# Ten attention heads instead of six with a second set of raw queries, and three operations placed elsewhere

## The chip, the cores and the metric

The kernel runs on one core of a Trainium2 chip. The metric is the device time of one execution in microseconds. TensorE (PE) multiplies matrices into eight PSUM banks of 128 x 512 floats; VectorE (DVE), ScalarE (ACT) and GpSimd (POOL) work element by element; SyncE (SP) and POOL issue transfers between on-chip memory and DRAM. Each engine takes its instructions in the order in which the program issues them, and waits at the first that isn't ready.

## The reference

One sequence of 2048 tokens of width 448 goes through an attention block with 16 heads of 28 columns and through a gated feed-forward block with a hidden width of 1792. A gate for each token mixes the two:

```python
qkv = (x @ wqkv).reshape(B, S, 3, H, Dh)
scores = einsum("bhqd,bhkd->bhqk", q, k) * Dh ** -0.5
a = softmax(scores) @ v ; a = a.reshape(B, S, D) @ wo
gate = x @ W_gate ; gate = gate * (gate > 0)
b = (gate * (x @ W_up)) @ W_down
g = sigmoid((x * gate_w).sum(-1))
out = g * a + (1 - g) * b
```

All is in 32-bit floats. Most products are made of a high part (rounded) and a low part (the rest), so that eleven matmuls (L116) stand for one product over 448 columns.

## The kernel before, in words

**Three stages.** The first (up to L635) splits x and the weights into high and low parts, makes queries, keys and values, writes them to DRAM, and begins on the row maxima. The second (L787 to L887) has 32 rounds, two for each head: an even round takes the first eight of the head's 16 blocks of 128 keys, an odd round the other eight. The third (from L893) is the rest of the feed-forward block, the output projection, and the result.

**A round's work.** Scores are made with keys in the partitions and 512 queries along the row (L309). The exponential needs each query's maximum first. For most queries the maxima come from a second, transposed product, queries by keys (`smax`, L282): one matmul for each 128 queries and 512 keys, and a maximum along the row on DVE (L284). They are made a head or so ahead. At the end of a head's maxima, `smax_end` transposes them on PE (L295), copies them on ACT (`mr`, L305), splits them into a high part on ACT (`mh`, L178) and a low part on DVE (`mh`, L184, by `low`), and SP writes both into two extra rows of the queries (L303), so that the score product subtracts them.

**Raw queries.** The last 512 queries (j = 3) go another way in every head but the first. Their raw scores for a round are made in the round before it, copied from PSUM by ACT (L321; in two late rounds by DVE, L319), and DVE keeps a running maximum over the key blocks (`raw_max`, L324). `raw_top` (L330 to L346) then makes one row of it on DVE, sends it through DRAM (`mr_d`) and spreads it over all partitions. In the round itself POOL subtracts it from each raw block (`raw_less`, L350) and ACT takes the exponential in place (`raw_exp`, L354). An odd round rescales what the even round has summed by a factor (`factors`, L369). In the heads of `WIDE` (L113) the odd round treats a second set of 512 queries (j = 2) in the same way: 16 raw blocks instead of eight, whose raw scores stand in the even round, and eight scores fewer in the odd one. Such a head needs only half of the maxima for its rows u from 8 to 11 (`parts_of`, L271), eight `smax` fewer.

**Products with v.** Each round ends with 64 matmuls of probabilities and values (`pv`, L728), four at a time in quarters of PE's columns, into bank 3. DVE copies the bank (L732) or adds it (L734). After an odd round POOL sends the row sums to DRAM and back in another shape (`ls`, L737). In the next even round, at the tenth score, DVE takes their reciprocals (`row_sums`, L745), and SP writes and spreads them (`spread`, L753). At the end of that round POOL multiplies (`normalise`, L758), and the normalised head goes to DRAM (`o_d`).

**Gate and up products.** Between these, PE works on the gate and up products of the feed-forward block (L690), in tiles of 2 x 11 matmuls. 55 of 56 tiles are made in the rounds, two in most and one in some; the hidden tile goes to DRAM (`h_d`, L712). Weights of the first 14 tiles are split by ACT and POOL in the early rounds.

**The order.** It is written out by hand in `ROUNDS` (L49), one string a round; a letter is an operation, a digit its bank: `s` a score and its exponential, `m` a row maximum, `r` a raw score and its copy, `d` a running maximum, `e` a raw exponential, `x` one gate-up matmul (20 of a tile's 22 stand in the string). The loop at L805 issues them one by one. `smax_end` of a head is issued at a round's start: the transpose and the copy at once, the split and the two transfers after the third and fourth score (L811). `raw_less` of all raw blocks is issued before the first letter (L799).

**The end.** After the last round one gate-up tile is left (`gate_up`, L954). The list `todo` (L1013) gives the order: that tile, the last head's row sums and spread, the splitting of wo (`split_wo`, L908), then 56 steps of the down product (`down`, L998; 12 matmuls of L985 a step), with `normalise` before step 3, the fetch of the normalised heads (`or`, L917) before steps 3, 8, 21 and 35, their splitting (`on`), and the output projection (`wout`, L939) in between. Each step fetches the h tile (and in the first 14 the w_down tile) four ahead (`fetch_d`, L964) and splits those two ahead on ACT and DVE (`split_d`, L972). For the last head, the row sums, the spread and the writing go over POOL's queue (`side`, L739).

Of the kernel before, what the change touches and what calls it, by code (L numbers as in the profile page):

```python
# [22 lines left out]
H = 16  # L23
# [34 lines left out]
    ("xxm0s7xm2s3m6xs7r1xm3s0m6s2xm1s3s7m0r6m2s1dm3xs7xxs0xm6s1r2m7xr3xs6xs1xxr0ddm6s7xr2dm3m1s6xxxxds7em0xm1xexm2"
     "m7xs3xs1xexm2xs3m7m1exs2xm0s3xexr1m2xs3m0xxs2xdxm0m3xxem1r2dxs0"),
    ("xr0xs7m2s1xm6s3xxxs0s2m3r1m7m6xs0xds3xs7xm0xs2m3s6xs7s1s2s3m6xxr7m1s0xds6em3r2xm1xxm7ds6r0s3xxxdxxs7em1m3xm2"  # L60
     "s0s7xxm1xexr3dxs2m0xxs1xexxr2edexxm3xxr0xdxs2"),
    ("xs1s0m6xs7m2xm1r3xr7m0s2xr3s1dm6xxr2s0dds7r1m6xxr3s0xds2dxs7r6xxxxm2s0s1xxs7xds0em3s6m2s7exm0xs1em3xs2m0xm7x"
     "m3xs0m1xs2em7xm0m3s1xxs2m7m0xm1xm2m3xxxs0xxexm1exm0r2xm3m1xxds0"),
    ("xs0r1m2s7m6xr3m0dxs1s2s6s7m0xxs3m1xm2xr0m6s1xdr7m2s3s6xdxs1m0xr2m3s6dxs7xs1xs0m3xs2r6m7m1s3xs0m2s7xs3r1dm0xd"
     "s2xexm3r7m6s0s2ds1e"),
    ("xs7s0m2s6xm1r3s7xm0m2s1s6xm3r0xs1xm7r2m6s3m1ds0r7xxxs3dr1xxs0s2ds3xm7r6m0dxxs2s3r1m7xs0xm6s2m7xr3xs6ds0m2dxx"
     "r1xdexxxr2s0xxr3dm7dxs1xs2xm0xs1m3r2xr0dxr1dr3xexxxxxr0ds2xexddm1"),
    ("xm7xr0m1r6m3xds2s7m0xs1xm2xs3s6m7xs0s1m3xxr6m2dm0xxs1r3xm2xr6xr1ds0xm2s7xxxxddxm3es0xs2m7xs1xm0xxem7m1exs3ee"
     "xem0xm2xs3xm0xm1xr2xxxxxdem0xr1m3s2xdxem0"),
# [1013 lines left out]
```

## Time and profile before

| | |
|---|---|
| median of 3 runs | 1237.44 us (1236.15 to 1240.22) |
| profiled execution | 1242.08 us, its span 1240.3 us |
| mean granted clock of TensorE | 0.992 |
| DMA queues 1 and 0 | 37.7% and 9.9% of 16 engines' span |
| row maxima on DVE (L284) | 736, 478.0 us busy |
| exponentials of scores on ACT (L311, into P) | 728, 403.1 us |
| gate and up matmuls (L690) | 1232, 404.1 us |
| raw subtractions on POOL (L350) | 288, in two groups of 211.3 and 150.8 us |

The profile lists for each engine the time in which some instruction of it was busy, for groups of instructions (source line, engine, tiles) their number, busy time and mean length, and the idle time of the engine just before them with what ended it. PE's instructions overlap: a matmul's row is longer than the distance to the next one. A row of a timeline gives start, length, engine, line, tiles and number of merged instructions; a row by stretch gives start and end of the stretch, its length, the busy time and number of instructions of each engine, the granted clock, DMA's share and rate.

### The profile page before, as it was taken

How to read it: one execution, taken by the hardware profiler on the slowest of the kernel's cores; microseconds unless marked ns; L12 is line 12 of the kernel's file. 1: busy time of each engine (PE TensorE's matmuls, PEld its weight loads, DVE VectorE, ACT ScalarE, POOL GpSimd, SP SyncE). 2: the span in 40 equal slices, each digit the busy share in tenths (PEclk: the TensorE clock that was granted, in tenths of full speed). 3: DMA queues.
4: the chain of work that ended last, by engine and by line, in shares of the span. 5: the costliest groups of instructions: out<-in, count | busy, mean ns of one | idle time of the engine just before them, and what ended most of it. 6: DMA issues, size and time to landing. Idle time of an engine off the chain costs nothing.

```text
span 1240.3 us, 18786 instructions
## 1 busy us (share of the span) xinstructions
PE 1214.4 (98%) x6399; PEld 868.3 (70%) x6399; DVE 922.1 (74%) x1622; ACT 816.6 (66%) x1615; POOL 548.8 (44%) x545
## 2 busy tenths in 40 slices
PE   9999999999979999999999999999999999899998
PEld 6888766666646666666666676666666666889997
DVE  6488876877787988889788888888888871543342
ACT  5312666788848787877888787878787885522121
POOL 4232325456553464374448454643738564400000
PEclk9999999999989999999999999999999999899999
DMA  8956736263627353435643443554342422753432
GB/s 305 345 209 247 249 130 214 84 195 99 210 68 250 106 163 100 131 125 163 202 155 108 155 127 106 164 158 144 122 163 86 149 88 81 244 180 110 137 105 77
DMA packets 68275, 193.99 MB, mean 156 GB/s; under 512 B 14850, under 2 KB 21602, under 8 KB 63754
## 3 DMA queue, kind: packets, MB, share of 16 engines
q1 hardware_dynamic: 55188, 148.02, 37.7%
q0 software_dynamic: 12560, 44.32, 9.9%
q8 instruction: 50, 0.82, 0.3%
q10 hardware_dynamic: 432, 0.46, 0.1%
q14 instruction: 45, 0.37, 0.1%
HBM read 132.09 MB, written 61.11 MB: 156 GB/s over the span
## 4 chain that ended last, share of the span: by engine, by line
PE 85%; DMA 6%; DVE 3%; POOL 2%; ACT 2%; issue 1%; SPq 0%; POOLq 0%; DVEq 0%; ACTq 0%
PE b L690 20%; PE b L728 17%; PE b L282 12%; PE b L309 12%; PE b L985 9%; PE b L503 5%; PE b L317 5%; DMA ls<-os 3%; PE b L521 3%; PE b L944 3%; POOL V L350 1%; DVE mx L284 1%; POOL wg L187 1%; DVE mh L184 1%; DMA or<-o_d 1%
## 5 line engine op out<-in xcount | busy, mean ns | idle before, releaser
L284 DVE TENSOR_REDUCE mx<-b 128x1 f32<-128x512 f32 x736 | 478.0, 684 | 44.6 <-PE b L282 40.0
L311 ACT ACTIVATE P<-b 128x512 f32<-128x512 f32 x728 | 403.1, 613 | 96.8 <-PE b L309 93.3
L690 PE MATMUL b<-X,wg 128*128 128x512 f32 (+1 forms) x1232 | 404.1, 401 | 0.3 <-POOL wg L187 0.3
L282 PE MATMUL b<-K,Q 128*128 128x512 f32 x736 | 281.1, 395 | 4.0 <-DVE mx L284 2.8
L309 PE MATMUL b<-Q,K 128*128 128x512 f32 x736 | 272.8, 395 | 3.6 <-DVE mx L284 2.6
L690 PEld LDWEIGHTS b<-X,wg 128*128 128x128 f32 (+1 forms) x1232 | 219.3, 188 | 69.9 <-issue 23.8
L350 POOL TENSOR_TENSOR V<-V,P 128x512 f32<-128x512 f32 x168 | 211.3, 1299 | 35.3 <-DMA P<-mr_d 17.4
L728 PE MATMUL b<-P,v 128*32 128x512 f32 x1696 | 226.3, 594 | 0.0
L712 POOL DMA_DIRECT2D h_d<-rl x56 | 31.3, 559 | 328.6 <-DVE rl L706 321.3
L309 PEld LDWEIGHTS b<-Q,K 128*128 128x128 f32 x736 | 139.0, 189 | 39.2 <-DVE mx L284 5.3
L282 PEld LDWEIGHTS b<-K,Q 128*128 128x128 f32 x736 | 138.6, 189 | 39.5 <-DVE mx L284 7.9
L324 DVE TENSOR_TENSOR P<-b,P 128x512 f32<-128x512 f32 x231 | 155.4, 681 | 11.0 <-ACT V L321 4.6
L350 POOL TENSOR_TENSOR P<-P,P 128x512 f32<-128x512 f32 x120 | 150.8, 1293 | 23.5 <-DMA P<-mr_d 18.5
L728 PEld LDWEIGHTS b<-P,v 128*32 128x32 f32 x1696 | 62.5, 110 | 124.6 <-issue 114.8
L985 PE MATMUL b<-WD,hh 128*128 128x448 f32 x672 | 142.9, 373 | 4.3 <-issue 3.8
L985 PEld LDWEIGHTS b<-WD,hh 128*128 128x128 f32 x672 | 128.2, 191 | 18.0 <-issue 4.1
L317 PE MATMUL b<-Q,K 128*128 128x512 f32 x288 | 111.8, 396 | 8.4 <-DVE mx L284 8.4
L728 PE MATMUL b<-V,v 128*32 128x512 f32 x352 | 114.4, 594 | 0.0
L178 ACT ACTIVATE hh<-hr 128x512 fp32r<-128x512 f32 x56 | 35.3, 631 | 113.3 <-PE b L985 112.6
L321 ACT ACTIVATE V<-b 128x512 f32<-128x512 f32 x160 | 93.6, 613 | 11.7 <-PE b L317 10.8
L354 ACT ACTIVATE V<-V 128x512 f32<-128x512 f32 x168 | 97.8, 663 | 0.0
L184 DVE TENSOR_TENSOR hh<-hr,hh 128x512 fp32r<-128x512 f32 x56 | 38.8, 693 | 63.4 <-ACT hh L178 63.1
(103 smaller groups left out, 1092.0 us busy)
## 6 DMA issues: line engine op xcount, KB each, us to landing
wg<-wgs_d SPq DMA_DIRECT2D x42, 896.0 KB
K<-qk_d SPq DMA_DIRECT2D x64, 224.0 KB
Q<-qk_d SPq DMA_DIRECT2D x64, 224.0 KB
h_d<-rl POOLq DMA_DIRECT2D x56, 256.0 KB, 3.8
hr<-h_d SPq DMA_DIRECT2D x56, 256.0 KB
wgs_d<-wg SPq DMA_DIRECT2D x14, 896.0 KB
qk_d<-st POOLq DMA_DIRECT2D x21, 512.0 KB, 4.7
wgr<-wgu SPq DMA_DIRECT2D x13, 512.0 KB
```

The costliest lines, as they stand in the source:

```text
L282: nc.tensor.matmul(ps, Q[h][:, u * P:(u + 1) * P], K[h % 3][:, c * TB:(c + 1) * TB], start=True, stop=True)
L284: nc.vector.tensor_reduce(MX[h][:, at:at + 1], ps, axis=AX.X, op=OP.max)
L309: nc.tensor.matmul(ps, K[h % 3][:, kt * P:(kt + 1) * P], Q[h][:, j * TB:(j + 1) * TB], start=True, stop=True)
L311: nc.scalar.activation(prob(i, j), ps, AF.Exp, scale=SCALE)
L317: nc.tensor.matmul(ps, K[h % 3][:, kt * P:(kt + 1) * P], Q[h][:, j * TB:(j + 1) * TB], start=True, stop=True)
L321: nc.scalar.activation(own, ps, AF.Copy)
L324: nc.vector.tensor_tensor(run(3 - j), ps, run(3 - j) if i % 8 > 1 else prob(i - 1, j), op=OP.max)
L350: nc.gpsimd.tensor_tensor(own, own, top(3 - j), op=OP.subtract)
L354: nc.scalar.activation(own, own, AF.Exp, scale=SCALE)
L690: nc.tensor.matmul(ps, WS[i][rows, s, a], xf(i // NF, b)[rows], start=(n == 0), stop=(n == NT - 1))
L728: nc.tensor.matmul(po[32 * j:32 * j + 32], VH[h][:, i % NK], prob(i, j), start=(i == i0), stop=(i == i0 + ni - 1))
L985: nc.tensor.matmul(ACC[i // NF][t][:, :D], HH[i][:, a, t * P:(t + 1) * P], WD[:, f, b], start=(f == 0 and n == 0), stop=(f == NF - 1 and n ...
```

## The change

`WIDE` grows from heads 4, 6, 8, 10, 12, 13 to heads 4 to 13. The strings of rounds 1 to 31 are all new; round 0 keeps its own. Counted over all strings, `s` goes from 720 to 688, `m` from 636 to 604, `r` from 288 to 320, `d` from 252 to 280, `e` from 138 to 154, and `x` stays at 1100. Rounds 10, 14, 18 and 22, now of wide heads, hold one gate-up tile instead of two, and the odd rounds after them two instead of one. Eight of the 32 fewer `m` are missing in round 5; the other 24 in rounds 10 to 23, six in each pair of rounds. The ten odd rounds from 9 to 27 now share one string (23 m, 16 s, 8 r, 40 x):

```diff
-WIDE = (4, 6, 8, 10, 12, 13)
+WIDE = (4, 5, 6, 7, 8, 9, 10, 11, 12, 13)
 # round 10
-    ("xs0m6s1m2r7xs0m3s1xs6m2m7r3xxdxs0r1m2s6xr3xdm7xxs0xds2s6r7xm3xm1ds0xs2s3m6xs1xs7m0xem6m3s2s1xxm7m6em2s3r0m1x"
-     "s7xs3dxr2xxs1xds7em3exm0xm1xm7s3xm0exm2r1m3xxxs0xdxxm2exm0xxm1xm2"),
+    ("s6s7m2s0m1s6xs3m2r7m0xr6m1r3m2s7m0r6xr1xds2r7dxs0xr3dxxxs6ds2r0dm1xs7m6xr3xdr1ds2s7xm6xds3s0m6s7m2s3s0m1r6xm"
+     "7s2ds3m0xr1s7xm2dr3xs6m0r7dxr2exr1ds6edees0d"),
```

The low part of the maxima goes to POOL, and all of `smax_end` is issued at the round's start:

```diff
             act_high(mh[:, 0], mr)
-            low(mh[:, 1], mr, mh[:, 0])
+            pool_low(mh[:, 1], mr, mh[:, 0])
...
-            rest = smax_end(min(M), banks[6])
-            rest.pop(0)()
+            for part in smax_end(min(M), banks[6]):
+                part()
```

The reciprocal of the row sums and its spread come at the sixteenth score of an even round:

```diff
-                if ns == 10 and r % 2 == 0 and h:
+                if ns == 16 and r % 2 == 0 and h:
                     row_sums(h - 1)
                     spread(h - 1)
```

In the end, row sums and spread come before step 1, the splitting of wo before steps 2 and 3, `normalise` and the first fetch of `or` before step 4; the first two pairs of w_down and h tiles are fetched before wo, and, as `start` is counted from `todo`, the first pair is split before the last gate-up tile:

```diff
-    todo = [(gate_up, done), (row_sums, H - 1), (spread, H - 1)] + [(gate_up, i) for i in range(done + 1, NB * NF)]
+    todo = [(gate_up, i) for i in range(done, NB * NF)]
...
-    before(3, (normalise, H - 1))
-    for tb, load, split, at in ((0, 3, (9, 10), (12, 12, 13, 13)), (1, 8, (12, 14), (17, 18, 19, 20)), (2, 21, (23, 25), (28,) * 4),
+    before(1, (row_sums, H - 1), (spread, H - 1))
+    before(4, (normalise, H - 1))
+    for c in range(4):
+        before(2 + c // 2, (split_wo, c))
+    for tb, load, split, at in ((0, 4, (9, 10), (12, 12, 13, 13)), (1, 8, (12, 14), (17, 18, 19, 20)), (2, 21, (23, 25), (28,) * 4),
...
-    todo[3:3] = [(split_wo, c) for c in range(4)]
-    load_wo()
     for i in range(4):
         fetch_d(i)
+        if i == 1:
+            load_wo()
```

More of the change, by code (lines that the diff above doesn't have):

```diff
@@ L58 @@
[L58 to L69, printed above, removed]
@@ new lines @@
+    ("xr7r1m0m6s2dxm3xs0r7xdm6xs1xs0m3xxs1r2m0r6xs3r1xdxs7xxdxs2dm3r6exxxs0xm7s3s1xds2m0em7s3xm1xxs0m2xs7m3s1xm2m0"
+     "es7xs3xs1m2s7xm3m0s1s2xem7m3xxm0s1m2xxm3xm1xr0xxdxexem2xs3xm0m1"),
+    ("xm7s2xm1s0xs6xm2s7m3s0xs6m1r7s2m3r0xm1s6r7s3s2dxm1xxs6s0xdm3s1m2r7m6xs0xs3xdm2s6m1r0s7m3xs2r6dxs1m7r3xds2s0x"
+     "m7xm1r6xs2xds0s7ede"),
+    ("xxr1m6s0xm7m3s2r1xr0xs6dm2s7dxxs3xxr1s7m6xxs2dm0m3s7es6xs1xm2m7xs3m0s6xxm2s1xem7m3s0m2xs6m7s1xs3m0xxs1m2xm3x"
+     "s7xm1s0xm3m7exm2s0xr3xxds1m0r2xxxdxs1em3m0xr2xdxr3xem1ds0xxm2ex"),
@@ new lines @@
+    ("xxs7m0xs2s1s6xm7xxs2s1m3s0s7m6r2xm1xxs0s3m6xr7s2r0xxm6ds1ds3xxs2m6er1xxs7xxxs0dxs3s2xes1m0xxxr3s7dxs2xr0xxxx"
+     "xedr3xeexs1dxxr0xxxm2s3xeds1x"),
+    ("xr0s1m7s2m6m3xxs1s7m0xm2s3m1xs7xm0s3r6m1xm7xxds0xs3s2xm7es1m6xr3xm7s2m0dxs6xxs7m1m0s2xxm7s6xm3r0dxs7r1xxem2s"
+     "3m7xxdxs2xm0s7m3xr2m1xm7er0xr3s1xxdexxexxs2xddm0xexm1xm2s3s0xm1"),
+    ("xm7s2xm1s0xs6xm2s7m3s0xs6m1r7s2m3r0xm1s6r7s3s2dxm1xxs6s0xdm3s1m2r7m6xs0xs3xdm2s6m1r0s7m3xs2r6dxs1m7r3xds2s0x"
+     "m7xm1r6xs2xds0s7ede"),
+    ("xs6r2m0s1r7m3xxr6xs2m1s0ds7xxs2xm0s1s7m3m6r2xs0m1s3dxxs7m6s0m1xr2xr7ds6dxs1m0xr3xexxr6ds1m2dxr7s0dxxm3r2xs1x"
+     "s0xs7xs1dm3m0r2dexr7xxds1xxs3r2m0xm1xexr3dxr0xxxddr2s1xm3xxm0xds1"),
@@ new lines @@
+    ("xs2m0m1r7s6xxm3m2r0ds7xxxs1xm2xr3s7m0xds6xr1xs0xds7s6m2xm0r3xm1xs2xs6dxm7s1m0m3r2xm7xxr0xm3xdxxxm1s3dexexm7x"
+     "xm2r3s1xs0xdxem2eexm1m3xxxxexm0em2xs3m1xe"),
+    ("xs6m1r7xm0r2xs3m7r1m6s2xr0dxs7xs2s3xdm6xs0m7s2m1s3r6xm7xdxs2m3r0s1xxr2dr6ds7dxxr0xm1dxm3s2xs7xs6m1r2xs7m0xds"
+     "3xm1s7xm0exr3xs2xs1dm7s0xr2xs1r3dexxxxdxm0s1r2xxr3xdxxr1dxdexm2s0"),
+    ("xs2m0m1r7s6xxm3m2r0ds7xxxs1xm2xr3s7m0xds6xr1xs0xds7s6m2xm0r3xm1xs2xs6dxm7s1m0m3r2xm7xxr0xm3xdxxxm1s3dexexm7x"
+     "xm2r3s1xs0xdxem2eexm1m3xxxxexm0em2xs3m1xe"),
@@ new lines @@
+    ("xs2m0m1r7s6xxm3m2r0ds7xxxs1xm2xr3s7m0xds6xr1xs0xds7s6m2xm0r3xm1xs2xs6dxm7s1m0m3r2xm7xxr0xm3xdxxxm1s3dexexm7x"
+     "xm2r3s1xs0xdxem2eexm1m3xxxxexm0em2xs3m1xe"),
+    ("r7r2m0r6s1m3s2xdm7r0r3s1xxddxr2s7m6xr1xdr0dxs6xr7xdm2s3xr6s1xdr0dxs3m2xdr7ds6xs1xs2m3m0s7s1m3s6m2s7m0s1xs6m2"
+     "s3m7r0xm6s1s2m3s7xxs6r1dm2m3exdr0r6s7edees2d"),
+    ("xs2m0m1r7s6xxm3m2r0ds7xxxs1xm2xr3s7m0xds6xr1xs0xds7s6m2xm0r3xm1xs2xs6dxm7s1m0m3r2xm7xxr0xm3xdxxxm1s3dexexm7x"
+     "xm2r3s1xs0xdxem2eexm1m3xxxxexm0em2xs3m1xe"),
@@ L111 @@
+    ("xxs0xs1xs3xxxs6s2s0s3xxxxs7s2s0s1xxs3xxxs6xs2xs7xxs1s3exxs0s2xxxxexs1s3xs0xexxxexxexxs2s0exxxx"),
 ]
-WIDE = (4, 6, 8, 10, 12, 13)
+WIDE = (4, 5, 6, 7, 8, 9, 10, 11, 12, 13)
 TERMS = [(0, 0), (3, 0), (1, 1), (4, 1), (2, 2), (5, 2), (6, 3), (0, 4), (1, 5), (2, 6), (6, 7)]
```

75 lines of the change are left out of this document (30 added, 45 removed).

## The prediction

> **What bounds the kernel now.** I read the page first, then the busy times by stretch. A stretch here is a round: from the first pv matmul (L728) of one round to the first of the next.
>
> ```profile
> span 1240.3 us, 18786 instructions
> PE 1214.4 (98%) x6399; PEld 868.3 (70%) x6399; DVE 922.1 (74%) x1622; ACT 816.6 (66%) x1615; POOL 548.8 (44%) x545
> ```
> ```profile
> core 0: us, PE busy (x) PEld busy (x) DVE busy (x) ACT busy (x) POOL busy (x), PEclk, DMA share, GB/s
> 192.93:227.64 34.71, 32.81 (x169) 21.80 (x168) 26.12 (x52) 24.33 (x50) 17.51 (x19) 0.95 0.57 199
> 251.47:285.14 33.67, 31.78 (x170) 21.13 (x168) 25.83 (x49) 27.74 (x56) 16.98 (x18) 1.00 0.54 173
> ...
> 345.43:379.65 34.22, 25.86 (x138) 16.55 (x137) 28.95 (x39) 19.63 (x43) 16.34 (x16) 0.85 0.42 142
> ...
> 494.18:524.92 30.74, 30.74 (x168) 21.45 (x166) 25.19 (x48) 26.86 (x54) 11.37 (x10) 1.00 0.41 126
> 524.92:552.67 27.75, 27.75 (x159) 18.33 (x157) 24.92 (x45) 21.23 (x44) 19.63 (x17) 1.00 0.36 119
> 552.67:583.36 30.69, 30.69 (x170) 20.87 (x169) 27.46 (x51) 26.21 (x51) 16.05 (x15) 1.00 0.54 164
> ...
> 998.87:1019.16 20.29, 20.29 (x121) 12.82 (x119) 14.00 (x28) 17.17 (x35) 12.33 (x11) 1.00 0.27 86
> ```
> ```profile
> 552.74 7.00 PE b L728 x64
> ```
>
> The rows are rounds 2, 4, 7, 12, 13, 14 and 30. PE is busy all through rounds 12 to 14, so a round is as long as its matmuls. Counting the letters s, m, r and x in the order strings gives 98, 87 and 100 of them, beside 64 pv matmuls in 7.0 us (the piece of the chain). Round 14 against round 13: (30.69 - 27.75) / (100 - 87) = 0.226 us for one matmul. It is issued at that pitch, though a row calls one 0.39 us long. So a round needs 7.0 + 0.226 x letters + about 0.5 for each gate-up tile. For 98 letters and two tiles that is 30.15, and round 12 has 0.6 over it; for 100 letters 30.6, and round 14 has 0.1. Three rounds lie far above: round 2 (99 letters, needs 30.4) by 4.3, round 4 (99) by 3.3, round 7 (69 letters, one tile, needs 23.1) by 11.1.
>
> ```profile
> 355.46 9.85 POOL L350 TENSOR_TENSOR V<-V,P 128x512 f32<-128x512 f32 x8
> ```
> ```profile
> 356.09 9.36 DVE L184 TENSOR_TENSOR mh<-mr,mh 12x128 fp32r<-12x128 f32 x1
> ```
> ```profile
> 366.11 0.80 PE L317 MATMUL b<-Q,K 128*128 128x512 f32 x1 [8.36 <-DVE mx L284]
> ```
> ```profile
> L178 ACT ACTIVATE mh<-mr x16: 290/293/309, 110.7 to 988.2; 12x128 fp32r<-12x128 f32 x15, 16x128 fp32r<-16x128 f32 x1
> L184 DVE TENSOR_TENSOR mh<-mr,mh x16: 269/777/9362, 111.3 to 988.5; 12x128 fp32r<-12x128 f32 x15, 16x128 fp32r<-16x128 f32 x1
> ```
>
> Three timelines and the tile mh tell of round 7. A subtraction of 12 by 128 on DVE, 0.27 us at its shortest, ran from 356.09 to 365.45, just past the end (365.31) of eight operations on POOL. Everything queued on DVE stood behind it, and PE sat 8.36 us for a bank that a row maximum had to free.
>
> ```profile
> DVE rs L745 <- DMA ls<-os: 12.8, 9, 2.8
> ```
> ```profile
> 211.43 0.25 DVE L745 RECIPROCAL rs<-ls 128x16 f32<-128x16 f32 x1 [2.76 <-DMA ls<-os]
> ```
>
> Waits and DVE's timeline tell of rounds 2 and 4: the reciprocal is issued at the tenth score matmul, before its transfer has landed, and DVE stands. Nine such waits hold DVE for 12.8 us.
>
> **The change, term by term.** The sum is made against the profiled execution, 1242.08 us, of which 1240.3 is the span; it lies 4.64 above the median of 1237.44. I keep 1242.08 as the base. How long the hold of round 7 lasts hangs on how two engines meet, so the timed runs may have had less of it; once it is gone, profiled and timed runs should agree, and I expect the median at the same figure.
>
> First, the matmuls. Heads 5, 7, 9 and 11 become wide; each drops eight row-maximum matmuls (m) and turns eight scores (s) into raw scores (r), which cost PE the same. The strings hold 604 m after 636, and 1100 x in both. 32 x 0.226 = 7.2 us less, all on the path since PE has no idle time there. **-7.2**
>
> Second, the subtraction of mh goes to POOL. Round 7 falls to what round 12 has over its need: 11.1 - 0.6. **-10.5.** It is weighed against a rule. The Trainium skill, page "SBUF — State Buffer", section "Who interferes with whom", says that a DVE instruction with two SBUF inputs contends with a GpSimd instruction that reads SBUF, and whichever issues second is blocked until the first finishes. By that, one POOL operation would be the most that mh waits for, and its move would be worth nothing in this sum: 1227 instead of 1216. The trace differs: mh was held through eight. What moving it costs: on POOL it is issued ahead of the raw subtractions (L350), and it waits for the maxima's transpose and two ACT copies of some 0.3 us each.
>
> ```profile
> L187 POOL TENSOR_TENSOR wg<-wgr,wg 64x128 fp32r<-64x128 f32 x26 | 11.9, 457 | 2.0
> ```
> ```profile
> 535.44 20.12 POOL L350 TENSOR_TENSOR V<-V,P 128x512 f32<-128x512 f32 x16 [3.00 <-ACT P L311]
> ```
> ```profile
> 554.47 3.24 ACT L354 ACTIVATE V<-V 128x512 f32<-128x512 f32 x6
> ```
>
> The nearest POOL row, 64 by 128, is 0.46 us; with the copies and the transpose mh is done some 1.4 us after pv ends (524.92 + 7.0), near 533.3, while L350 starts at 535.44 anyway. So nothing, with 2 us of cover; beyond that each us late pushes the chain below.
>
> Third, the reciprocal at the sixteenth score. By the new strings that is at letter 51 or later of a full round, 11.5 us after pv ends. In round 2, the latest, the transfer landed 211.4 - 199.9 = 11.5 us after pv's end; its sixteenth s is letter 59, 13.3 us. So the wait goes. On SP the four spreads wait behind it, and behind them the next weights' fetch and the maxima of the raw rows; the shortest of these rounds has 26 letters or 5.9 us left, and the result (L758) is wanted only after it. Worth between the PE idle of the rounds 2 and 4 (34.71 - 32.81 + 33.67 - 31.78 = 3.8) and the 12.8 of DVE; I take the middle, since rounds 2 and 4 alone lie 7.6 over. **-8**
>
> Fourth, rounds 10, 14, 18 and 22 have one gate-up tile (77 letters) and the rounds behind them two (87, like round 13). In the short rounds ACT gets 24 s, 16 r and 4 exponentials (e) in the 17.9 us between two pv stages.
>
> ```profile
> 1007.74 7.62 ACT L311 ACTIVATE P<-b 128x512 f32<-128x512 f32 x15
> ```
> ```profile
> 213.58 1.88 DVE L284 TENSOR_REDUCE mx<-b 128x1 f32<-128x512 f32 x3
> ```
>
> ACT's pitch: (7.62 - 0.61) / 14 = 0.50; an exponential of a raw row (3.24 - 0.64) / 5 = 0.52. 40 x 0.50 + 4 x 0.52 = 22.1, so ACT ends 4.2 behind PE. DVE has 17 m and 14 running maxima at (1.88 - 0.68) / 2 = 0.60, with the copy of pv's bank 19.2, 1.3 behind. Round 30 is the nearest: 52 letters, 12.3 us, ACT 32 x 0.50 + 2 x 0.52 = 17.0, 4.7 behind, and it lies 20.29 - 19.25 = 1.0 over its need: the eight banks and the next pv stage take up most of it. The new rounds have DVE late as well, so I take 1.4 over the need where the rounds now have 0.6; the ends are no loss and the whole 4.2. Four times 0.8: **+3.** The four two-tile rounds behind them cost what round 13 does, nothing over its need. The cover there is thin: POOL's 16 subtractions end at 555.56, the last exponential at 557.71, and pv (552.67 + 7.0) wants the last block near 558.8. 32 more subtractions at 1.25 us and 32 exponentials lie in it.
>
> Fifth, the end.
>
> ```profile
> 1048.59 5.28 PE L690 MATMUL b<-X,wg 128*128 128x512 f32 x22
> 1057.63 32.18 PE L985 MATMUL b<-WD,hh 128*128 128x448 f32 x144 [3.75 <-issue]
> ```
> ```profile
> 1041.00:1048.70 7.70, 7.70 (x70) 2.31 (x69) 2.48 (x4) 2.19 (x5) 1.13 (x2) 1.00 0.18 68
> 1052.00:1056.00 4.00, 1.88 (x9) 1.22 (x7) 0.94 (x2) 1.53 (x4) 0.64 (x2) 1.00 1.01 317
> 1056.00:1060.00 4.00, 2.37 (x6) 2.04 (x7) 2.83 (x5) 3.42 (x7) 0.47 (x1) 0.60 1.04 363
> 1060.00:1064.00 4.00, 4.00 (x13) 3.59 (x12) 2.43 (x5) 2.00 (x4) 2.21 (x5) 0.54 0.89 298
> ```
> ```profile
> 1055.37 0.25 DVE L745 RECIPROCAL rs<-ls 128x16 f32<-128x16 f32 x1 [0.71 <-DMA ls<-os]
> ```
> ```profile
> 1063.22 5.72 DMA rb<-l_d
> ...
> 1088.27 5.68 DMA hr<-h_d
> ```
>
> PE stands 3.75 us before the first down product, and the granted clock is then 0.60 and 0.54, which costs about 0.40 x 2.4 + 0.46 x 4 = 2.8 more: 6.5 in all. The change fetches two wd and two h tiles ahead of wo, where DMA is idle (share 0.18) if their space is free by then, and splits the first pair before the last gate-up. That closes the gap. But a chain ends later than PE: row sums, l_d, rb, normalise, o_d, or, and the refetch of hr at 1088.27. The reciprocal now stands behind two more pairs of splits on DVE, four operations of 0.6 behind 1054.6, so near 1057.2 instead of 1055.4, 1.8 later. Against that, two of each tile,
>
> ```profile
> hr<-h_d SPq DMA_DIRECT2D x56, 256.0 KB
> ```
> ```profile
> wdr<-wd SPq DMA_DIRECT2D x14, 224.0 KB
> ```
>
> 960 KB at some 300 GB/s, 3.2 us, leave the full DMA stretch in which this chain's transfers wait. Ends: +2 (later, no relief) and -6.5 (the whole gap). I take about half, since the chain decides: **-3.**
>
> Sum: -7.2 - 10.5 - 8 + 3 - 3 = -25.7, and 1242.1 - 25.7 = 1216.4.
>
> **Rivals.** Short rounds bound by ACT: the whole 4.2 is paid in each, 4 x (4.2 - 1.4) = 11 more, 1228. For it: 22.1 us of work in 17.9. Against it: round 30. The hold stays: DVE's delay in round 7 was not POOL's doing and only its place moves; 10.5 back, 1227. Against it: the two ends 0.14 us apart. The rule of the Trainium skill's page "SBUF — State Buffer" above points this way, since it lets one POOL operation hold DVE and not eight. The reciprocal still waits: the transfer lands later behind the extra work on POOL, which issues it; 8 back, 1224. Its margin in round 2 is 1.8 us. Slower: the raw subtractions of a short round run into the DVE subtraction L345 at its end, which also reads two SBUF tiles, and hold it as they held mh, 9.4 us. That decides from the third of the four rounds on, as 3 x 9.4 exceeds 25.7; at four it gives 1254 with nothing else lost. Against it: if the raw subtractions start as in round 13, 10.5 us into the round (535.44 - 524.92), eight end at 20.6 of 25.4, some 5 us before, and L345 was held in none of 15 places, as its mean says.
>
> ```profile
> L345 DVE TENSOR_TENSOR row_a<-row_a,row_b 32x32 f32<-32x32 f32 x15 | 2.7, 179 | 0.5
> ```
>
>
> **How the numbers follow.** Forecast 0.64; short rounds 0.14; hold 0.06; reciprocal 0.09; slower 0.03; other 0.04. 1216.4 rounds to 1216. The range 1206 to 1229 takes in the first four: below, 8 for the reciprocal could be 12.8 and the end 6.5, together 8 better, and the two further us for short rounds without loss; above, the short rounds at full price. What a measurement tells from no change is about 0.3%, 3.7 us. Same needs two rivals together: 0.04. Slower 0.04, faster 0.92.
>
> **What would show it.** Right: 704 maxima on L284 (736 now), no mh on DVE, round 7 near 23.7, no DVE idle time at L745 before the last head, short rounds near 26.3, the gap before L985 under 1 us. Wrong: PE idle over 2 us in rounds 10, 14, 18 or 22 ended by ACT, or PE waiting in the end for hh behind rb or hr. The forecast falls if the rounds together shorten by less than 15 us.

## The result, and the profile after

The changed kernel takes 1221.05 us, median of four runs (1218.93 to 1221.39); the kernel before, in four runs beside it, 1238.83 (1236.15 to 1243.40). The ratio is 0.985, with an interval from 0.982 to 0.988. The profiled execution is the one of 1218.93, so against the profile of before, 1242.08, it is 23.2 shorter; the forecast was 25.7 shorter. The median lies 5 us over the predicted 1216, inside the range.

First the page of after, where PE has 32 fewer matmuls (6399 before) and no longer a share of 98%, and one group of its fifth part.

```profile
span 1217.2 us, 18787 instructions
PE 1201.5 (99%) x6367; PEld 859.1 (71%) x6367; DVE 910.8 (75%) x1606; ACT 831.2 (68%) x1647; POOL 593.8 (49%) x593
...
L284 DVE TENSOR_REDUCE mx<-b 128x1 f32<-128x512 f32 x704 | 458.6, 686 | 50.1 <-PE b L282 44.6
```

Then the busy times by stretch, after, for rounds 2, 4, 7, 10, 11, 14 and 15, cut as in the prediction from the first pv matmul of one round to that of the next.

```profile
core 0: us, PE busy (x) PEld busy (x) DVE busy (x) ACT busy (x) POOL busy (x), PEclk, DMA share, GB/s
192.81:223.56 30.75, 30.75 (x169) 20.61 (x167) 25.78 (x51) 23.78 (x49) 17.56 (x19) 1.00 0.66 224
246.99:278.87 31.88, 31.64 (x170) 20.73 (x168) 25.68 (x48) 27.84 (x56) 17.03 (x18) 1.00 0.56 183
...
336.30:359.80 23.50, 23.50 (x139) 15.06 (x137) 19.58 (x39) 18.94 (x42) 16.95 (x17) 1.00 0.50 167
419.50:445.66 26.16, 26.14 (x145) 16.06 (x143) 23.42 (x45) 23.79 (x50) 16.32 (x15) 1.00 0.60 191
445.66:474.30 28.64, 28.64 (x159) 18.73 (x157) 25.43 (x46) 23.23 (x47) 20.23 (x18) 1.00 0.22 75
532.51:558.75 26.24, 26.24 (x146) 15.90 (x144) 23.74 (x45) 23.86 (x50) 16.30 (x15) 1.00 0.60 192
558.75:587.05 28.30, 28.30 (x158) 19.73 (x157) 25.35 (x46) 23.10 (x47) 19.46 (x17) 1.00 0.33 98
```

Round 2 fell from 34.71 to 30.75, round 4 from 33.67 to 31.88, round 7 from 34.22 to 23.50. The tile mh of after shows where the held subtraction went, and the groups show the reciprocal without idle time before it:

```profile
L187 POOL TENSOR_TENSOR mh<-mr,mh x16: 448/452/456, 112.4 to 965.6; 12x128 fp32r<-12x128 f32 x15, 16x128 fp32r<-16x128 f32 x1
```
```profile
L745 DVE RECIPROCAL rs<-ls 128x16 f32<-128x16 f32 x16 | 3.9, 243 | 0.0
```

Where the 23.1 us of span went: from round 1 to the last pv stage 880.3 before (161.27 to 1041.59) and 858.6 after (161.16 to 1019.80), 21.7 less; behind the last pv stage's start 198.7 and 197.4, 1.3 less; the first stage 0.1. So nearly all of it is in the rounds, and the new end brought little.

The waits of after name one that grew (total, number, longest):

```profile
DVE P L330 <- POOL V L350: 18.8, 10, 3.5
```

PE's timeline of after shows two of the new waits in the rounds, the first in round 16, the second in round 22, and SP's and DVE's timelines what was late.

```profile
606.14 0.47 PE L282 MATMUL b<-K,Q 128*128 128x512 f32 x1 [1.13 <-DMA wg<-wgs_d]
...
767.27 0.74 PE L317 MATMUL b<-Q,K 128*128 128x512 f32 x2 [0.94 <-DMA mr_d<-row_a]
```
```profile
592.45 0.33 SPq L343 DMA_DIRECT2D mr_d<-row_a  x1
596.66 0.34 SPq L346 DMA_DIRECT2D P<-mr_d  x1
597.05 3.10 SPq L260 DMA_DIRECT2D Q<-qk_d  x4
...
600.67 0.81 SPq L679 DMA_DIRECT2D wg<-wgs_d  x2
```
```profile
762.34 0.71 DVE L330 STREAM_TRANSPOSE P<-P 128x512 f32<-128x512 f32 x1 [2.88 <-POOL V L350]
...
765.95 1.26 DVE L706 TENSOR_TENSOR rl<-b,rl 128x512 f32<-128x512 f32 x2
```

In round 16 the gate-up weights were fetched at 600.67, since on SP they stand behind the spread of the raw maxima (L346), which waits until the row (L343, issued at 592.45) is in DRAM, and behind the queries of a later head (L260). PE wanted them some 4 us later and stood for 1.13; in round 24 it stood 0.51 in the same way. In round 22 the row's releaser isn't the cause: the first raw score wants bank 7, and DVE freed that bank at 767.21 with L706, itself behind the row of raw maxima (L330 and what follows), which had waited 2.88 us for POOL. PE started 0.06 us later. The wait for POOL at L330 stood 9.0 us in all before; now it is 18.8, as in four more heads the row of maxima shares its time with raw subtractions.

The end, in the timelines of PE and DVE of after:

```profile
1031.94 5.03 PE L985 MATMUL b<-WD,hh 128*128 128x448 f32 x24
1038.15 10.70 PE L985 MATMUL b<-WD,hh 128*128 128x448 f32 x49 [1.18 <-ACT hh L178]
1051.91 16.61 PE L985 MATMUL b<-WD,hh 128*128 128x448 f32 x71 [3.06 <-DVE WD L184]
```
```profile
1037.40 0.63 DVE L184 TENSOR_TENSOR WD<-wdr,WD 128x448 fp32r<-128x448 f32 x1 [3.21 <-ACT WD L178]
...
1038.74 0.24 DVE L745 RECIPROCAL rs<-ls 128x16 f32<-128x16 f32 x1
...
1050.36 0.96 DVE L758 TENSOR_TENSOR os<-os,rb 128x512 f32<-128x512 f32 x1 [5.14 <-DMA rb<-l_d]
```

The gap of 3.75 us before the first down product is gone: it starts right behind the last gate-up tile. But PE stands 1.18 and then 3.06 us later on, and 1.56 once more at 1074.54, where before has one wait of 0.47 behind its gap. In the longest of them the split that PE wants stands on DVE behind `normalise`, and `normalise` stood 5.14 us for rb. And rb is late because the reciprocal, whose row sums had landed 12.1 us after the last pv stage's start (1031.9), ran only at 1038.74.

### The profile page after: what moved, and what is told of

Same layout as the page of the kernel before. It is cut to its first block, busy times and chain, and to the rows that moved or that the text cites. A ratio compares the mean times of both kernels' runs of the same rounds, so it can differ in the third digit from the quotient of the medians.

```text
span 1217.2 us, 18787 instructions
## 1 busy us (share of the span) xinstructions
PE 1201.5 (99%) x6367; PEld 859.1 (71%) x6367; DVE 910.8 (75%) x1606; ACT 831.2 (68%) x1647; POOL 593.8 (49%) x593
## 4 chain that ended last, share of the span: by engine, by line
PE 75%; DMA 8%; POOL 6%; ACT 6%; DVE 4%; issue 1%; SPq 1%; DVEq 0%; POOLq 0%; ACTq 0%
PE b L690 16%; PE b L728 14%; PE b L282 10%; PE b L309 10%; PE b L985 9%; PE b L503 6%; POOL V L350 5%; PE b L317 4%; ACT P L311 3%; PE b L521 3%; PE b L944 3%; DMA P<-mr_d 2%; ACT V L321 1%; DMA hr<-h_d 1%; DMA wg<-wgs_d 1%
## 5 line engine op out<-in xcount | busy, mean ns | idle before, releaser
L284 DVE TENSOR_REDUCE mx<-b 128x1 f32<-128x512 f32 x704 | 458.6, 686 | 50.1 <-PE b L282 44.6
L311 ACT ACTIVATE P<-b 128x512 f32<-128x512 f32 x696 | 392.0, 634 | 67.5 <-PE b L309 64.4
L350 POOL TENSOR_TENSOR V<-V,P 128x512 f32<-128x512 f32 x200 | 251.0, 1292 | 28.2 <-DMA P<-mr_d 25.8
L282 PE MATMUL b<-K,Q 128*128 128x512 f32 x704 | 262.1, 394 | 1.5 <-DMA wg<-wgs_d 1.1
L324 DVE TENSOR_TENSOR P<-b,P 128x512 f32<-128x512 f32 x255 | 171.4, 684 | 13.0 <-ACT P L321 6.7
L309 PEld LDWEIGHTS b<-Q,K 128*128 128x128 f32 x704 | 131.8, 188 | 38.5 <-ACT P L311 2.9
L728 PEld LDWEIGHTS b<-P,v 128*32 128x32 f32 x1632 | 66.9, 110 | 130.2 <-issue 111.6
L282 PEld LDWEIGHTS b<-K,Q 128*128 128x128 f32 x704 | 132.1, 188 | 35.4 <-ACT V L321 2.1
L321 ACT ACTIVATE V<-b 128x512 f32<-128x512 f32 x192 | 115.9, 642 | 28.5 <-PE b L317 27.1
L354 ACT ACTIVATE V<-V 128x512 f32<-128x512 f32 x200 | 112.7, 655 | 0.2 <-POOL V L350 0.2
```

The costliest lines, as they stand in the source:

```text
L282: nc.tensor.matmul(ps, Q[h][:, u * P:(u + 1) * P], K[h % 3][:, c * TB:(c + 1) * TB], start=True, stop=True)
L284: nc.vector.tensor_reduce(MX[h][:, at:at + 1], ps, axis=AX.X, op=OP.max)
L309: nc.tensor.matmul(ps, K[h % 3][:, kt * P:(kt + 1) * P], Q[h][:, j * TB:(j + 1) * TB], start=True, stop=True)
L311: nc.scalar.activation(prob(i, j), ps, AF.Exp, scale=SCALE)
L321: nc.scalar.activation(own, ps, AF.Copy)
L324: nc.vector.tensor_tensor(run(3 - j), ps, run(3 - j) if i % 8 > 1 else prob(i - 1, j), op=OP.max)
```

## The experiments

Where a median is given, it is compared with runs of before on the same chip, whose median is 1238.32 for e1 to e4, 1239.78 for e5 to e8 and 1239.89 for e10. After was measured on yet another chip, with 1238.83 for before; where two medians of different chips are set against each other, 1 or 2 us of the difference can be the chips'. Lengths of rounds are those of the profiled execution.

### The subtraction alone on POOL, at the round's start (e1_mh_on_pool)

```diff
 # on the kernel before
-            low(mh[:, 1], mr, mh[:, 0])
+            pool_low(mh[:, 1], mr, mh[:, 0])
...
-            rest = smax_end(min(M), banks[6])
-            rest.pop(0)()
+            for part in smax_end(min(M), banks[6]):
+                part()
```

> The kernel before with one edit: the low part of mh on POOL, and all of it at the round's start. Theory (DVE was held by POOL's run of raw subtractions): round 7 shrinks from 34.2 us to about 23.5, no other round grows, and the time falls by 8 to 11 us, to about 1229. Rival (the hold had another cause and only moves): round 7 stays above 30 us or another round grows by 8 or more, and the time stays within 3 us of before.

1227.07, that is 11.3 less; ratio 0.9913 (0.9889 to 0.9936). Busy time by stretch of this kernel, its round 7:

```profile
343.15:366.58 23.43, 23.43 (x138) 14.97 (x136) 19.49 (x39) 19.14 (x43) 16.96 (x17) 1.00 0.46 161
```

34.22 before, so 10.8 less, and no other round grew by more than 1.7 us. The move is worth what the hold cost.

### The row sums alone at the sixteenth score (e2_sums_at_16)

```diff
 # on the kernel before
-                if ns == 10 and r % 2 == 0 and h:
+                if ns == 16 and r % 2 == 0 and h:
```

> The kernel before with one edit: reciprocal and spread of the row sums at the sixteenth score. Theory: rounds 2, 4 and 6 shrink by 6 to 8 us together and 26 and 28 by about 1 each, 8 us in all, to about 1231. Rival (the later place delays the weights' fetch that stands behind it on SP): PE waits for wg by a DMA in several rounds, 1 us or more each, and less than 4 us is left of the gain.

1229.88, 8.4 less; ratio 0.9930 (0.9905 to 0.9955). Round 2 fell to 30.71, with PE busy all through it, round 4 to 31.47, round 28 from 25.89 to 24.44; round 7 kept its 34.31. Nothing came to wait for what now stands later on SP.

### The new end alone (e3_new_end)

```diff
 # on the kernel before
-    todo = [(gate_up, done), (row_sums, H - 1), (spread, H - 1)] + [(gate_up, i) for i in range(done + 1, NB * NF)]
+    todo = [(gate_up, i) for i in range(done, NB * NF)]
...
+    before(1, (row_sums, H - 1), (spread, H - 1))
+    before(4, (normalise, H - 1))
...
     for i in range(4):
         fetch_d(i)
+        if i == 1:
+            load_wo()
```

> The kernel before with the new order of the end alone. Theory: the gap of 3.75 us before the first down product closes, but the chain of the last head's row sums gives it back as waits of PE later, so the stretch behind the last pv is 1 to 2 us shorter than 198.7 and the time falls by 1 to 2 us. Rival (the end is worth what the gap and the slow clock cost): 5 to 6.5 us less.

1243.53, 5.2 more; ratio 1.0034 (1.0014 to 1.0054). Both theories expected no loss, so both fell; the gap closed and came back as later waits, as the theory had it, but as more than the gap. The stretch behind the last pv stage's start is 200.1 where before has 198.7. DVE's and PE's timelines of this kernel (its last pv stage starts at 1043.6):

```profile
1064.12 0.24 DVE L745 RECIPROCAL rs<-ls 128x16 f32<-128x16 f32 x1
```
```profile
1063.53 10.70 PE L985 MATMUL b<-WD,hh 128*128 128x448 f32 x49 [1.68 <-ACT hh L178]
1076.58 3.71 PE L985 MATMUL b<-WD,hh 128*128 128x448 f32 x15 [2.35 <-DVE WD L184]
```

The same two waits as in after: the reciprocal 20.5 us into the stretch (13.8 before), `normalise` at 1075.30 behind it, and PE's second wait behind `normalise`.

### Ten wide heads and their strings alone (e4_ten_heads_alone)

```diff
 # on the changed kernel: the three other parts put back
-            pool_low(mh[:, 1], mr, mh[:, 0])
+            low(mh[:, 1], mr, mh[:, 0])
...
-                if ns == 16 and r % 2 == 0 and h:
+                if ns == 10 and r % 2 == 0 and h:
...
-    todo = [(gate_up, i) for i in range(done, NB * NF)]
+    todo = [(gate_up, done), (row_sums, H - 1), (spread, H - 1)] + [(gate_up, i) for i in range(done + 1, NB * NF)]
...
```

> The changed kernel with the three operations put back to their old places: the ten heads and the new strings alone. Theory: 32 matmuls less are worth 7.2 us, the short rounds 10, 14, 18 and 22 give back 4 to 5, so it is 2 to 3 us faster than before if mh is held as long as it was; and as the hold depends on where POOL and DVE meet, the time can lie up to 11 us lower or some 10 to 20 higher, with mh rows on DVE of several us wherever it does. Rival (the ten heads carry the gain): 1224 or less with mh still on DVE and the reciprocal still waiting.

1251.06, 12.7 more; ratio 1.0088 (1.0057 to 1.0119). 32 fewer matmuls, and yet slower: in the profiled execution DVE's subtraction was held twice, 9.76 us in round 3 and 9.43 in round 7, and these rounds are 35.66 and 34.67 long where after has 23.43 and 23.50. The new strings don't only keep the hold, they bring a second one, and without the move to POOL the change would have been a loss. One of the seven executions took only 1239.0; it wasn't traced.

### The subtraction back on DVE at its old place (e5_mh_late_on_dve)

```diff
 # on the changed kernel
-            pool_low(mh[:, 1], mr, mh[:, 0])
+            low(mh[:, 1], mr, mh[:, 0])
...
-            for part in smax_end(min(M), banks[6]):
-                part()
+            rest = smax_end(min(M), banks[6])
+            rest.pop(0)()
```

> The changed kernel with the low part of mh back on DVE at its old place behind the third score. In the runs so far a DVE subtraction of mh that began inside a POOL subtraction ended 0.14 us after that one, or, in rounds 3 and 7, 0.14 us after the last of eight; the held ones met a POOL operation that had followed its predecessor within 1.251 us, all others one that had stood before. Theory: held in rounds 3 and 7, not from round 9 on, where POOL waits 3 us or more for the spread maxima; 10 to 21 us slower than the changed kernel. Rival (any of the runs can hold it): a hold of more than 2 us in a wide round.

1247.0; ratio 1.0045 (1.0018 to 1.0072), some 25 us over after, more than the 10 to 21 expected. Eight of ten runs lie between 1245.5 and 1250.5, two at 1235.0 and 1236.6; only one execution was traced, so whether those two had one hold less isn't shown. DVE's timeline and POOL's of this kernel, in round 3:

```profile
233.90 9.78 DVE L184 TENSOR_TENSOR mh<-mr,mh 12x128 fp32r<-12x128 f32 x1 [0.89 <-ACT mh L178]
```
```profile
229.44 3.04 POOL L187 TENSOR_TENSOR wg<-wgr,wg 128x384 fp32r<-128x384 f32 x4
232.45 1.28 POOL L758 TENSOR_TENSOR os<-os,rb 128x512 f32<-128x512 f32 x1
233.70 9.83 POOL L350 TENSOR_TENSOR V<-V,P 128x512 f32<-128x512 f32 x8
```

POOL's run ends at 243.53, DVE's operation at 243.68, 0.14 behind its eighth operation and not behind its first. From the last of the splits on (232.03), POOL had run without a pause through `normalise` and all eight subtractions. Of the others none was held over 1.35 us: DVE was let in 0.14 us behind the one POOL operation that it had met, and in all but one of these cases POOL had stood for some 2 to 3 us just before. The one is round 5, which the expectation had overlooked: POOL had run 2.0 us without a pause there, and paused 0.08 us behind the operation that DVE met. So the hold belongs to rounds 3 and 7, in which POOL's weight splitting runs into its subtractions.

Such a run doesn't always hold DVE. In e2_sums_at_16, POOL's timeline and DVE's in round 3 show the same run, and DVE was let in behind the first raw subtraction:

```profile
229.38 3.04 POOL L187 TENSOR_TENSOR wg<-wgr,wg 128x384 fp32r<-128x384 f32 x4
232.39 1.28 POOL L758 TENSOR_TENSOR os<-os,rb 128x512 f32<-128x512 f32 x1
233.65 10.12 POOL L350 TENSOR_TENSOR V<-V,P 128x512 f32<-128x512 f32 x8
```
```profile
234.23 0.85 DVE L184 TENSOR_TENSOR mh<-mr,mh 12x128 fp32r<-12x128 f32 x1
```

### Early, but still on DVE (e6_mh_early_on_dve)

```diff
 # on the changed kernel: only the engine put back
-            pool_low(mh[:, 1], mr, mh[:, 0])
+            low(mh[:, 1], mr, mh[:, 0])
```

> The changed kernel with the low part of mh on DVE, but issued at the round's start. Theory (the place decides as much as the engine): DVE gets there before the raw subtractions begin in all rounds from 9 on, so no hold; in rounds 3, 5 and 7 it meets POOL's splitting of weights, each under 1.3 us; within 3 us of the changed kernel. Rival (it must be off DVE): at least one hold of 8 us or more and a time of 1229 or more.

1233.14; ratio 0.9953 (0.9933 to 0.9973), 12 over after. One hold is left, in round 7, and it is the longest of all. DVE's timeline and POOL's:

```profile
344.25 11.48 DVE L184 TENSOR_TENSOR mh<-mr,mh 12x128 fp32r<-12x128 f32 x1
```
```profile
341.54 3.04 POOL L187 TENSOR_TENSOR wg<-wgr,wg 128x384 fp32r<-128x384 f32 x4
344.55 1.29 POOL L758 TENSOR_TENSOR os<-os,rb 128x512 f32<-128x512 f32 x1
345.80 9.79 POOL L350 TENSOR_TENSOR V<-V,P 128x512 f32<-128x512 f32 x8
```

It met the last split at 344.25 and was let in at 355.73, behind the split, `normalise` and eight subtractions, ten operations, although POOL had paused 0.08 us just before that split. So the theory fell and the rival held: an earlier place on DVE doesn't end the holds, another engine does.

### The changed kernel with the old end (e7_old_end)

```diff
 # on the changed kernel: the end put back
-    todo = [(gate_up, i) for i in range(done, NB * NF)]
+    todo = [(gate_up, done), (row_sums, H - 1), (spread, H - 1)] + [(gate_up, i) for i in range(done + 1, NB * NF)]
...
+    load_wo()
     for i in range(4):
         fetch_d(i)
-        if i == 1:
-            load_wo()
```

> The changed kernel with the old order of the end. Theory: the new end closes the gap before the first down product, but sets the last head's reciprocal behind the third pair of splits on DVE, 5 us later than needed, and the chain behind it hands that on to PE; with the old end the stretch behind the last pv is 194.6 instead of 197.4, so 2 to 3 us faster than the changed kernel, near 1218.5. Rival (the new end is worth its gap): 2 us or more slower than the changed kernel.

1215.02 (1214.72 to 1217.85); ratio 0.9808 (0.9790 to 0.9827). It is the fastest kernel of the study: 6 us under after in the medians, 5 by the two ratios, whose intervals overlap a little. PE's timeline, DVE's, and the busy times by stretch of this kernel (last pv stage from 1021.04):

```profile
1036.99 31.09 PE L985 MATMUL b<-WD,hh 128*128 128x448 f32 x144 [3.62 <-issue]
```
```profile
1034.16 0.25 DVE L745 RECIPROCAL rs<-ls 128x16 f32<-128x16 f32 x1
...
1047.11 1.61 DVE L758 TENSOR_TENSOR os<-os,rb 128x512 f32<-128x512 f32 x1 [1.18 <-DMA rb<-l_d]
```
```profile
1037.00:1043.40 6.40, 6.40 (x24) 5.48 (x25) 4.83 (x8) 4.12 (x8) 2.41 (x5) 0.73 1.00 346
```

The gap is back, 3.62 us, and the slow clock behind it. But the reciprocal stands 13.1 us into the stretch (18.9 in after) and `normalise` 26.1 (30.6); then PE runs 144 matmuls in a row, where after stands for another 3.06. The stretch is 195.0 long, against 197.4. In the medians the new end costs 6.0 here and 5.2 in e3_new_end; in the profiles 2.3 and 1.4. All traces with the new strings agree in sign: the stretch is 194.6 to 195.8 in the three with the old end (e4, e7, e10) and 197.4 to 203.0 in the six with the new end and its late reciprocal (after, e5, e6, e9, e11, e12).

### New end, row sums first (e8_sums_first)

```diff
 # on the changed kernel
-    before(1, (row_sums, H - 1), (spread, H - 1))
+    before(0, (row_sums, H - 1), (spread, H - 1))
...
-    start = todo.index((down, 0)) - 1
+    start = (0, todo.index((down, 0)))
...
-        if n in (start, start + 1):
-            split_d(n - start)
+        if n in start:
+            split_d(start.index(n))
```

> The changed kernel with the last head's row sums and spread straight behind the last gate-up tile, ahead of the second pair of splits; the rest of the new end kept. Theory: the reciprocal starts near 13 us behind the last pv instead of 18.9, the gap stays closed, the stretch behind the last pv falls from 197.4 to 191 to 193, and the time by 4 to 6 us, to about 1216. Rival (the chain is bound by the transfers, not by the reciprocal): less than 2 us.

1218.17 (1214.49 to 1220.08); ratio 0.9827 (0.9805 to 0.9849). The reciprocal is back at 13.3 us into the stretch and PE begins the down products at 1031.44, right behind the last gate-up tile. PE's timeline of this kernel, with the three longest waits of the end:

```profile
1034.41 3.02 PE L985 MATMUL b<-WD,hh 128*128 128x448 f32 x12 [0.37 <-ACT hh L178]
1038.96 8.66 PE L985 MATMUL b<-WD,hh 128*128 128x448 f32 x38 [1.53 <-ACT hh L178]
...
1071.40 3.02 PE L985 MATMUL b<-WD,hh 128*128 128x448 f32 x12 [2.09 <-ACT hh L178]
```

With a fourth of 0.34 before 1047.97 they come to 4.3 us together, where the old end has 3.62 and 0.95. The stretch is 194.7, within 0.3 of the old end's, where 191 to 193 were expected. The down products begin earlier, but PE's later waits are for splits of their tiles, and ACT, which splits them, stood up to 8.5 us for a w_down tile; what is gained at the front is given back within 40 us. In the profiled execution the late reciprocal is the whole loss of the new end, and without it there is no gain either. In the medians e8 lies halfway, 3 us under after and 3 over e7_old_end, so about half of the loss isn't explained there.

### No pause before the subtractions (e9_no_gap)

Why are only rounds 3 and 7 held? This kernel tests whether it needs POOL to come to the raw subtractions without a pause, by one short operation ahead of them, into a tile that nobody reads.

```diff
 # on e5_mh_late_on_dve
+        if exps:
+            junk = keep.tile([P, 64], F32, name=f"junk_{r}", tag="junk", bufs=1)
+            nc.gpsimd.tensor_tensor(junk, top(0)[:, :64], top(0)[:, :64], op=OP.subtract)
         for i, j in exps:
             raw_less(i, j)
```

> The kernel of e5 (low part of mh on DVE behind the third score) with one short POOL subtraction of 64 columns, into a tile that nothing uses, ahead of each round's raw subtractions: it waits for the spread maxima in their place, so that the first raw subtraction follows a POOL operation without standing. Theory (a hold lasts to the end of POOL's run when the run is entered without a pause): holds of 9 us or more also in wide rounds from 9 on, where e5 had none over 1.35 us, up to 20 us each; the time is 1260 or more. Rival (only rounds 3 and 7 have it, by their splitting of weights or their 8 narrow blocks): no hold over 1.5 us from round 9 on, and within 10 us of e5.

1247.27, one execution. Held 10.03 us in round 3 and 9.64 in round 7, and never over 1.05 from round 9 on, although the subtractions there now followed an operation 0.25 us before. The theory fell: one operation ahead doesn't make the run that holds.

### Eight short operations ahead (e12_train)

```diff
 # on e9_no_gap
-            nc.gpsimd.tensor_tensor(junk, top(0)[:, :64], top(0)[:, :64], op=OP.subtract)
+            for _ in range(8):
+                nc.gpsimd.tensor_tensor(junk, top(0)[:, :64], top(0)[:, :64], op=OP.subtract)
```

> The kernel of e9 with eight short POOL subtractions of 64 columns ahead of each round's raw subtractions instead of one, so that POOL has about 2 us of unbroken work behind it when it reaches them. In all runs so far the held subtractions met POOL after several operations without a pause (splitting of weights, normalise, raw subtractions), those let in met it one or two operations behind a pause. Theory (a train of several operations keeps DVE out to its end): holds of 9 us or more in wide rounds from 9 on. Rival (it is the place or the kind of the operations ahead in rounds 3 and 7): again none over 1.5 us from round 9 on, and what decides stays open.

1248.24, one execution, and the holds are gone everywhere, in rounds 3 and 7 too. The tile mh of this kernel, and DVE's and POOL's timelines in round 3:

```profile
L184 DVE TENSOR_TENSOR mh<-mr,mh x16: 270/280/516, 111.7 to 992.5; 12x128 fp32r<-12x128 f32 x15, 16x128 fp32r<-16x128 f32 x1
```
```profile
234.42 0.28 DVE L184 TENSOR_TENSOR mh<-mr,mh 12x128 fp32r<-12x128 f32 x1 [0.89 <-ACT mh L178]
```
```profile
234.23 2.88 POOL L802 TENSOR_TENSOR junk<-P 128x64 f32<-128x64 f32 x8
```

The short operations are 0.29 long and 0.37 apart, so POOL pauses 0.08 us after each, and DVE, which began inside the first, was done in its usual 0.28 us. That is the opposite of what was meant: a train of operations with such pauses lets DVE in, where the run of e5_mh_late_on_dve didn't. The time is lost elsewhere: round 10 is 28.50 long, 26.16 in after, with 5 us more of POOL's work in it.

### The weights' fetch ahead of the queries (e10_weights_first)

The waits of after for wg seemed to come from SP's order. This kernel has the old end and turns that order round.

```diff
 # on e7_old_end
-        if r % 2 and h + 3 < H:
-            load_q(h + 3)
         for _ in range(2):
             next_w()
+        if r % 2 and h + 3 < H:
+            load_q(h + 3)
```

> The changed kernel with the old end, and in odd rounds the next gate-up weights fetched ahead of the next queries on SP. Theory: PE's waits for wg in rounds 16 and 24 (1.3 and 0.7 us in the changed kernel) go, as the fetch no longer stands behind four query transfers of 0.75 us of issue each; 1 to 3 us faster than the old end alone, near 1213. Rival (the fetch is late because the spread maxima's transfer stands ahead of it, or DMA is full): within 1 us of the old end alone.

1269.07; ratio 1.0229 (1.0206 to 1.0253), 54 us over e7_old_end. Neither theory had that. The waits of this kernel:

```profile
PE b L282 <- DMA Q<-qk_d: 37.4, 9, 6.3
```

The fetch of the weights waits on SP until their buffer is free, up to 9.7 us, and the queries now wait behind it: PE stood for them in the even rounds from 8 to 24, up to 6.3 us at a time. That is 37.4 of the 54 us; behind eight of these nine waits the granted clock was 0.50 for 3.4 or 6.8 us, and its mean is 0.977 (0.998 in e7_old_end). The old order costs after 1.6 us of waiting for weights and keeps the queries on time.

### Less for ACT or for DVE in the short rounds (e11_short_rounds)

This kernel leaves out part of the computation: the exponentials of the raw rows in rounds 10 and 18, and 12 of the 14 running maxima in rounds 14 and 22.

```diff
 # on the changed kernel
-                raw_max(*tops.pop(0))
+                t = tops.pop(0)
+                if r not in (14, 22) or t[0] % 8 < 2:
+                    raw_max(*t)
...
-                raw_exp(*exps.pop(0))
+                e = exps.pop(0)
+                if r not in (10, 18):
+                    raw_exp(*e)
...
+        exps = [] if r in (10, 18) else exps
```

> The changed kernel with work left out in its four short rounds: in rounds 10 and 18 the exponentials of the raw rows on ACT (8 of 0.52 us), in rounds 14 and 22 all running maxima on DVE but the first two (12 of 0.60 us). The changed kernel has 1.2, 1.4, 1.2 and 2.4 us over the need in rounds 10, 18, 14 and 22. Theory (ACT is late most): rounds 10 and 18 fall to 0.5 or less over their need, 14 stays at 0.8 or more. Rival (DVE, or banks held for the running maxima): round 14 falls to 0.5 or less and 10 and 18 stay at 0.8 or more. If neither falls, it is the dependencies at the round's edges.

1220.36, one execution. The stretches of this kernel for rounds 10, 11 and 14:

```profile
419.92:446.14 26.22, 26.19 (x146) 16.07 (x144) 23.48 (x45) 23.84 (x50) 16.50 (x15) 1.00 0.61 192
446.14:473.95 27.81, 27.81 (x158) 18.43 (x157) 25.35 (x46) 19.04 (x39) 18.62 (x17) 1.00 0.24 76
532.78:559.02 26.24, 26.17 (x146) 15.77 (x144) 19.14 (x37) 23.86 (x50) 16.29 (x15) 1.00 0.58 193
```

Round 14 keeps its 26.24 with 4.6 us less for DVE (19.14, 23.74 in after), so DVE's load isn't what lengthens it. Round 10 keeps its 26.2 too, but ACT's time in it doesn't fall (23.84): in after seven of the eight exponentials begin behind its end. They come out of round 11, where ACT falls from 23.23 to 19.04 and the round from 28.64 to 27.81; round 19, behind round 18, falls by only 0.1. So the raw exponentials cost the short round nothing and the next one 0.8 or 0.1. What makes the 1.2 us that the short round has over its need isn't told apart: PE's timeline of after lists no wait there, but eight matmuls of round 10 begin 0.3 to 0.4 us behind the one before, where 0.23 is usual, and ACT's exponentials of scores and its copies were not lightened here.

## Why the prediction was right, and where not

**Fewer matmuls, -7.2.** Right by the count (6399 to 6367, 736 row maxima to 704), but little of it came as time. Round 5, which loses eight, fell from 28.6 to 26.6, 2.0 where 1.8 was expected (to 27.2 with mh on DVE, in e4_ten_heads_alone). Rounds 10 to 23 lose the other 24, 5.4 us, and were to give 3 back in the short rounds; they got no shorter at all: from the pv stage of round 9 to that of round 23 it is 395.6 us before (439.19 to 834.84) and 395.6 after (419.50 to 815.07). What took it is told under the short rounds and the waits for weights. So of the 21.7 us gained in the rounds, 19.2 come from the two operations put elsewhere, 10.7 and 8.5, and only some 2.5 from the rest, the ten heads and their strings among it.

**The subtraction of mh, -10.5.** Right in mechanism and size: 10.7 in the profile (34.22 to 23.50) and 11.3 in the medians of e1_mh_on_pool. The rule of the Trainium skill, page "SBUF — State Buffer", section "Who interferes with whom", by which DVE waits only for the first GpSimd instruction that it meets, is what most holds show (0.14 us behind the end of that one operation). In rounds 3 and 7 the measurement differs from it: held through eight to ten operations, up to 11.48 us, and here the measurement decides. What the prediction missed is that the new strings would have made two holds of one (e4_ten_heads_alone, e5_mh_late_on_dve): against the new strings on DVE the move is worth some 25 us (1247.0 against 1221.05, each with before on its own chip), not 10.5.

**The reciprocal, -8.** Right: rounds 2, 4, 6, 26 and 28 together 8.5 shorter in the profile, 8.4 in the medians of e2_sums_at_16; the wait row has gone. The middle of the two bounds held.

**The short rounds, +3.** The size held: rounds 10, 14, 18 and 22 are 26.16, 26.24, 26.38 and 27.41 long, 106.2 together against 105.2 expected. Of the reason one half held and one fell. ACT ends late, and the pv stage takes it up, as expected: seven of the eight raw exponentials of round 10 begin behind the round's end. But that DVE's lateness costs the round something on top is wrong, as less work for DVE changed nothing. And "nothing over its need" for the two-tile rounds behind them was wrong by 2.2 us in four rounds (28.64, 28.30, 27.89 and 28.41 against 27.75 each): part of ACT's late work is paid there, 0.8 us in round 11 and 0.1 in round 19, as e11_short_rounds shows; the rest wasn't tested. The 1.1 us by which round 22 exceeds the other three is a wait for a bank that DVE frees late behind the row of raw maxima; the prediction looked at that chain for a hold (its slower rival) and not for this.

**The waits for weights.** Not in the prediction: 1.6 us in rounds 16 and 24, behind the queries on SP.

**The end, -3.** This step failed, in sign. The stretch fell by 1.3 us in the profile, but that isn't the new end's doing: with the old end the same kernel is shorter (197.4 against 195.0, and 6 us in the medians), and alone it costs before 5.2. The prediction set the reciprocal behind "two more pairs of splits on DVE, four operations of 0.6", 1.8 later; that counted the operations of DVE and not what they wait for. The third pair is queued ahead of the reciprocal as well, its w_down tile comes behind wo on SP, and so DVE stood 3.21 us at 1037.40 while the row sums lay ready. The reciprocal came 18.9 us into the stretch, 5.1 later than before instead of 1.8, and pushed rb, `normalise` and the splits behind `normalise`, up to PE. With the reciprocal first (e8_sums_first) the loss is gone in the profile and half gone in the medians. Of the relief of 3.2 us that was set against it the trace shows 2.1: from the reciprocal to the last of rb it takes 11.5 us, 13.6 before. The text had named the sign of it, PE waiting in the end behind rb; it is there, with 3.06 us.

**Why the old end is shorter in the new kernel than in before** (195.0 against 198.7) is settled only in part. Behind the same gap the granted clock is 0.50 for 6.8 us in the profile of before and for 3.4 in those of e1, e2, e4 and e7, which is worth 1.7 us. What decides its length stays open, and so does the rest: e1 and e2, with the old strings and 3.4 us of low clock, still have 197.8 and 197.3.

**The sum.** Rounds -21.7 against -22.7, end -1.3 against -3. That profiled and timed runs would agree held to 2.1 us (1218.93 and 1221.05). The difference of the medians is smaller, 17.8, since the median of before lies some 3 to 5 us under its profiled execution. Counted from the median of before, 1238.83, the same terms give 1213, 8 us under the measured 1221, and the end alone accounts for that, with 5 to 6 more where 3 less was forecast. That the high base hid part of it is luck.

## What to carry to other kernels

Before an operation is put ahead of a chain on an in-order engine, follow what that operation itself waits for: the new end was 5 to 6 us slower, and about half of that or more because three pairs of splits, the third with a late transfer, went ahead of one reciprocal whose data lay ready. A stall at one place can be closed and be given back within a few tens of us where transfers set the pace, so a reordering should be timed alone, as here, where the best kernel is the change without one of its parts. And an operation of 0.3 us can cost 10 where DVE meets POOL in a run without pauses: look for groups whose longest row is far from the median, and move the operation to the other engine, not to another time.
